# Two of three matrix products of a mixture layer by seven products on token halves, with its weight sums kept in DRAM

## Chip, core and metric

The kernel runs on one core of a Trainium2 chip. The metric is the device time of one execution in microseconds; several runs are taken, and their median counts. One execution was also profiled; all rows below are of that one.

## The reference

Attention in two steps (32 packed queries per head attend to the sequence, then the sequence attends to the 32 results), its output laid out as 4608 tokens of 512, and two feed-forward layers. The second is the one that is changed. Its weights and those of the first come as float64.

```python
p_packed = sm_attn(p, k, v)
out = sm_attn(q, p_packed, p_packed)                 # 8 batches, 8 heads, 576 tokens, 64
x = out.transpose(0, 2, 1, 3).reshape(4608, 512)
h = x @ w_in                                          # 512 -> 2048
g = np.where(h > 0.0, h, np.exp(np.minimum(h, 0.0)) - 1.0)
x2 = g @ w_out                                        # 2048 -> 512
a, b = x2 @ w_a, x2 @ w_b                             # 512 -> 1536 each
result = (a * b) @ w_out2                             # 1536 -> 512
```

## The kernel before

**Arithmetic.** Each large product is made of values split in two fp32r parts, hi and lo, and three matmuls (hi x hi, hi x lo, lo x hi) stand for one. Making a hi part is a cast on ACT, making the lo part a subtraction on DVE or POOL (`split`, L78; `convert`, L118 to L151). A float64 weight tile of 128 x 512 comes in as pairs of 32-bit words (512 KB, `load_words`), and `convert` makes it float32 with ACT, DVE and POOL steps u0 to u2; u3 makes hi and lo.

**Phase 1** goes batch by batch (eight blocks, about 85 us each from block 1 on; 288 tokens are one half of a batch). For each half and each of 16 pieces f of the hidden 2048, `l1` makes h (L466, 6 matmuls of 288 columns), `act1` makes g from it (ACT L474 and L475, DVE L478 for gf, ACT L480 and DVE L482 for gr) and `l2` adds its 12 matmuls into the four x2a banks (L488), two steps later. The attention of the next batch runs between these steps. Its work is put at due times: `put(t, fn)` queues a function for step time t, `run_until(t)` issues what has come due, with 2 time units for one step (h, f). The softmax over the packed keys (L331 to L358) and the transposes of the next batch's keys (L222) are DVE work of this kind. x2 goes to DRAM (x2d) as transposed tokens.

**Phase 2** takes nine blocks of 512 tokens and twelve pieces f of the hidden 1536. `l3` makes a and b of a piece (L727, 12 matmuls of 512 columns each), ACT copies a (L733), DVE multiplies by b (L735), and the product is split into cr (ACT L79, DVE L80). `l4` of the piece before adds its 12 matmuls into four banks o (L747). After piece 11 ACT and DVE copy the four banks into output tiles, which have two buffers (L758, L760), and SP stores them.

**Weights of phase 2.** There are 36 tiles (a, b, o of each f). All stay in SBUF, in slots that come free as phase 1 ends, so nine are converted during block 7 and 27 at the start of phase 2 (the list `convs`, at times T7 and T8, where the first unit of block 7 and the end of phase 1 lie).

The order on each engine is that of a scheduler that works from the program's order; a DMA issue on SP waits in line like any instruction.

## Time and profile before

| | us |
|---|---|
| median of 3 runs (lowest, highest) | 1731.46 (1731.41, 1734.84) |
| the profiled execution | 1731.33 |
| its span, first to last instruction | 1729.6 |
| PE busy, DVE busy, ACT busy, POOL busy | 1653.1, 796.5, 664.0, 160.7 |
| mean granted TensorE clock | 0.977 |

Busy times are sums over the span, and stages differ: POOL is busy only in the first stage and around the seam of the phases, DVE more in phase 1 than in phase 2. Matmuls are pipelined: the length of one in the profile holds time that it shares with its neighbours, so a pace is read from the starts of groups. Line numbers are those of the code above.

### The profile page before, as it was taken

The numbers are of one execution on the slowest core, as the hardware profiler recorded it, in microseconds if no ns is written. First come the engines' busy times: TensorE is split into PE (matmuls) and PEld (weight loads), VectorE is DVE, ScalarE is ACT, GpSimd is POOL, SyncE is SP. The second block draws the span as 40 slices with busy tenths as digits, with TensorE's granted clock in tenths as the row PEclk, the third lists the DMA queues.
The fourth block names the chain that finished last, engine by engine and source line by source line (L and its number), as shares of the span: only waits on it lengthen the run. The fifth ranks groups of instructions, "written<-read, shape, count | busy, mean of one in ns | idle before, by whom it ended". The sixth has DMA issues, their size and how long they took to land.

```text
span 1729.6 us, 25599 instructions
## 1 busy us (share of the span) xinstructions
PE 1653.1 (96%) x10392; PEld 1407.3 (81%) x10392; DVE 796.5 (46%) x1579; ACT 664.0 (38%) x1440; POOL 160.7 (9%) x124
## 2 busy tenths in 40 slices
PE   5489999999999999999989999999999999999998
PEld 3378889898989899898768888888888888888886
DVE  6998674656565655786892121221212121121211
ACT  4575655555656565565432121211212121121111
POOL 2564000000000000232450000000000000000000
PEclk7599999999999999999989999999999999999999
DMA  7754222223232221022531010010101000000000
GB/s 219 191 153 118 61 56 59 54 57 56 57 56 57 56 79 34 26 87 93 165 119 52 1 43 7 6 43 0 49 1 49 1 25 25 0 31 1 25 0 25
DMA packets 194806, 96.82 MB, mean 56 GB/s; under 512 B 147584, under 2 KB 179328, under 8 KB 194688
## 3 DMA queue, kind: packets, MB, share of 16 engines
q1 hardware_dynamic: 194688, 95.19, 20.2%
...
## 4 chain that ended last, share of the span: by engine, by line
PE 80%; DVE 12%; DMA 3%; issue 2%; SPq 1%; ACT 1%; POOL 1%; DVEq 0%; ACTq 0%; POOLq 0%
PE x2a L488 18%; PE o L747 17%; PE a L727 16%; PE b L727 16%; PE h L466 9%; DVE gf L478 1%; PE pp L294 1%; DVE kT L222 1%; DVE gr L482 1%; DMA wst_2b<-in_moe_w_b_dram 1%; DMA wst_i<-in_moe_w_in_dram 1%; DVE qT L222 1%; DVE wm_2b L135 0%; DVE t L337 0%; DMA wst_o<-in_moe_w_out_dram 0%
## 5 line engine op out<-in xcount | busy, mean ns | idle before, releaser
L488 PE MATMUL x2a<-gr,wout 128*128 128x288 f32 x3072 | 473.0, 300 | 10.6 <-DVE gr L482 6.6
L488 PEld LDWEIGHTS x2a<-gr,wout 128*128 128x128 f32 x3072 | 428.8, 190 | 43.4 <-issue 17.8
L735 DVE TENSOR_TENSOR cf<-asb,b 128x512 f32<-128x512 f32 x108 | 74.2, 687 | 533.1 <-PE b L727 532.4
L466 PE MATMUL h<-a,wr 128*128 128x288 f32 x1536 | 260.5, 304 | 21.8 <-DVE gf L478 14.1
L466 PEld LDWEIGHTS h<-a,wr 128*128 128x128 f32 x1536 | 222.8, 192 | 44.1 <-DVE gf L478 20.6
L733 ACT COPY asb<-a 128x512 f32<-128x512 f32 x108 | 63.4, 587 | 388.8 <-PE a L727 388.8
L727 PE MATMUL a<-x2r,wout 128*128 128x512 f32 x864 | 209.0, 391 | 0.0
L727 PEld LDWEIGHTS a<-x2r,wout 128*128 128x128 f32 x864 | 163.0, 189 | 35.9
L478 DVE SCALAR_TENSOR_TENSOR gf<-ge,h 128x288 f32<-128x288 f32 x256 | 114.6, 448 | 138.4 <-ACT ge L475 135.9
L79 ACT CAST cr<-cf 128x512 fp32r<-128x512 f32 x108 | 67.0, 620 | 249.2 <-DVE cf L735 249.2
L480 ACT CAST gr<-gf 128x288 fp32r<-128x288 f32 x256 | 110.3, 431 | 119.9 <-DVE gf L478 119.1
L474 ACT ACTIVATE ge<-h 128x288 f32<-128x288 f32 x256 | 104.9, 410 | 134.0 <-PE h L466 133.6
L482 DVE TENSOR_TENSOR gr<-gf,gr 128x288 fp32r<-128x288 f32 x240 | 115.4, 481 | 69.2 <-ACT gr L480 67.4
L747 PE MATMUL o<-wr,cr 128*128 128x512 f32 x540 | 138.9, 406 | 8.3 <-DVE cr L80 4.8
L747 PEld LDWEIGHTS o<-wr,cr 128*128 128x128 f32 x540 | 103.7, 193 | 35.3 <-DVE cr L80 6.5
L727 PE MATMUL b<-x2r,wr 128*128 128x512 f32 x540 | 129.8, 389 | 0.0
L727 PEld LDWEIGHTS b<-x2r,wr 128*128 128x128 f32 x540 | 101.4, 188 | 21.0
L475 ACT ACTIVATE ge<-ge 128x288 f32<-128x288 f32 x256 | 113.7, 445 | 5.5
L747 PE MATMUL o<-wout,cr 128*128 128x512 f32 x432 | 107.2, 396 | 0.2 <-DVE cr L80 0.2
L727 PE MATMUL a<-x2r,wx 128*128 128x512 f32 x432 | 104.2, 390 | 0.0
L80 DVE TENSOR_TENSOR cr<-cf,cr 128x512 fp32r<-128x512 f32 x108 | 76.8, 711 | 58.8 <-ACT cr L79 58.8
L727 PE MATMUL b<-x2r,wout 128*128 128x512 f32 x432 | 103.8, 389 | 0.0
...
## 6 DMA issues: line engine op xcount, KB each, us to landing
...
v<-in_v_dram SPq DMA_DIRECT2D x8, 1024.0 KB, 5.7
wst_i<-in_moe_w_in_dram SPq DMA_DIRECT2D x16, 512.0 KB, 5.3
wst_o<-in_moe_w_out_dram SPq DMA_DIRECT2D x16, 512.0 KB, 4.1
kst<-in_k_dram SPq DMA_DIRECT2D x112, 72.0 KB, 2.4
qst<-in_q_dram SPq DMA_DIRECT2D x112, 72.0 KB, 2.4
wst_2a<-in_moe_w_a_dram SPq DMA_DIRECT2D x12, 512.0 KB, 4.3
```

The source lines that it names most:

```text
L79: nc.scalar.copy(hi, src)
L80: nc.vector.tensor_tensor(lo, src, hi.bitcast(F32), op=ALU.subtract)
L466: nc.tensor.matmul(t[:, :HS], w[:, wi, o * P:(o + 1) * P], x[:, xi, :], start=(n == 0), stop=(n == 5))
L474: nc.scalar.activation(e, t[:, :HS], AF.Relu, scale=-1.0)
L475: nc.scalar.activation(e, e, AF.Exp, scale=-1.0)
L478: nc.vector.scalar_tensor_tensor(g, e, -1.0, t[:, :HS], op0=ALU.add, op1=ALU.max)
L480: nc.scalar.copy(gr[:, 0, :], g)
L482: (nc.gpsimd if pool_lo else nc.vector).tensor_tensor(gr[:, 1, :], g, gr[:, 0, :].bitcast(F32), op=ALU.subtract)
L488: nc.tensor.matmul(acc[d][:, :HS], wout_r[f][:, wi, d * P:(d + 1) * P], gr[:, xi, :], start=(first and n == 0), stop=(last and n == 2),)
L727: nc.tensor.matmul(t, w[:, wi, d * P:(d + 1) * P], xr[blk, d][:, xi, :], start=(n == 0), stop=(n == 3 * NDM - 1))
L735: nc.vector.tensor_tensor(c, a, ab[1], op=ALU.mult)
L747: nc.tensor.matmul(acc[t], cr[:, xi, t * P:(t + 1) * P], w[:, wi, :], start=(f == 0 and n == 0), stop=(f == NF2 - 1 and n == 2),)
```

## The change

Phase 2 is rewritten. Tokens are taken in six groups of 768, two halves of 384. For each piece f, [x2 halves] x [w_a | w_b] is a product of 2 x 2 blocks (two token halves, two halves of the 512 input channels; a and b). Strassen's scheme in Winograd's form makes the four block results from seven block products instead of eight: each product is one combination of token blocks (seven tensors s, made once a group) times one combination of weight blocks (seven tensors e, made once for each f). A product is six matmuls of 384 columns (two channel pieces of 128, three hi/lo terms). Sums of products are built in three PSUM banks A, B, C and on DVE (u, v, w), and then c1 = a x b of one half and c2 of the other are split as before. `l4` uses c1 of three token tiles right after, the tiles of c2 and the rest in a tail of 117 matmuls at the end of a group.

All 36 weight tiles are converted to float32 in blocks 1 to 6 of phase 1, one each 10 units, and stored in DRAM (wf). In group 0 the combinations e of a piece are made from them (`e_make`: 4 subtractions on DVE, 3 casts on ACT, 3 subtractions on POOL), stored in DRAM (ed, 1792 KB for each f), and groups 1 to 5 load them again (`e_load`, two buffers). Some buffers of the conversions in block 0 are also taken from other pools.

```diff
+            def u4():
+                nc.sync.dma_start(store, m.bitcast(F32))
...
+        GAP = (T7 - 4 * NF - 24) / len(w2src)
...
+        def w2_step(i, n):
+            kind, f, _ = w2src[i]
+            if n == 0:
+                w2words[i] = convert(w2words[i], f"2{kind}{f}", (stage, 2), store=wf[kind, f])
+            w2words[i][n]()
+
+        for i in range(len(w2src)):
+            t = 4 * NF + 12 + GAP * i
+            put(t - 7, w2_load, i)
+            for n, dt in enumerate((0, 1, 2, 5)):
+                put(t + dt, w2_step, i, n)
...
+        def e_load_words(f):
+            for kind in "ab":
+                t = stage.tile([P, 512], F32, tag="wmag", name=f"wl{kind}{f}", bufs=2)
+                nc.sync.dma_start(t, wf[kind, f])
+                wst2[kind, f] = t
+
+        def e_make(f):
+
+            a, b = wst2.pop(("a", f)), wst2.pop(("b", f))
+            e = p2.tile([P, 7, 2, 2 * P], F32R, tag="e2", name=f"e2_{f}", bufs=2)
+            c = stage.tile([P, 4, 2 * P], F32, tag="wst", name=f"wc{f}")
+            h1, h2 = slice(0, 2 * P), slice(2 * P, 4 * P)
+            nc.vector.tensor_tensor(c[:, 0, :], b[:, h1], a[:, h1], op=ALU.subtract)
+            nc.vector.tensor_tensor(c[:, 1, :], b[:, h2], b[:, h1], op=ALU.subtract)
+            nc.vector.tensor_tensor(c[:, 2, :], b[:, h2], c[:, 0, :], op=ALU.subtract)
+            nc.vector.tensor_tensor(c[:, 3, :], a[:, h2], c[:, 2, :], op=ALU.subtract)
+            for i, n, src in ((0, 2, a.rearrange("p (n x) -> p n x", n=2)), (2, 1, b[:, None, h2]), (3, 4, c)):
+                nc.scalar.copy(e[:, i:i + n, 0, :], src)
+                nc.gpsimd.tensor_tensor(e[:, i:i + n, 1, :], src, e[:, i:i + n, 0, :].bitcast(F32), op=ALU.subtract)
+            nc.sync.dma_start(ed[f], e.bitcast(F32))
+            es[f] = e
...
+        def e_load(f, g):
+            e = p2.tile([P, 7, 2, 2 * P], F32R, tag="e2", name=f"e2_{g}_{f}", bufs=2)
+            nc.sync.dma_start(e.bitcast(F32), ed[f])
...
+        def s_part(g, i, src):
+            s = p2.tile([P, 2, 2 * HT], F32R, tag=f"s{i}", name=f"s{i}_{g}")
+            split(s[:, 0, :], s[:, 1, :], src)
...
+            if step == 0:
+                s_part(g, 1, x11)
+                s1 = stage.tile([P, 2 * HT], F32, tag="wst", name=f"x2s1_{g}")
+                xs[g, "s1"] = s1
+                nc.vector.tensor_tensor(s1, x21, x22, op=ALU.add)
+                nc.vector.tensor_tensor(x21, x11, x21, op=ALU.subtract)
+                nc.vector.tensor_tensor(x11, s1, x11, op=ALU.subtract)
+                s_part(g, 6, x11)
+            elif step == 1:
+                s_part(g, 5, xs[g, "s1"])
+                s_part(g, 2, x12)
+                s_part(g, 7, x21)
+            else:
+                nc.vector.tensor_tensor(x12, x12, x11, op=ALU.subtract)
+                s_part(g, 3, x12)
+                s_part(g, 4, x22)
...
+        put(T7 + 4, e_load_words, 0)
+        put(T7 + 14, e_make, 0)
+        put(T7 + 20, e_load_words, 1)
+        put(T7 + 30, e_make, 1)
+        put(T7 + 36, e_load_words, 2)
+        put(T7 + 36, x_load, 0)
+        for n in range(3):
+            put(T7 + 46 + 4 * n, s_make, 0, n)
...
+        def o_load(f):
+            t = p4.tile([P, 512], F32, tag="wol", name=f"wlo{f}")
+            nc.sync.dma_start(t, wf["o", f])
+            w = p4.tile([P, 2, 512], F32R, tag=f"wo{f}", name=f"wo{f}", bufs=1)
+            nc.scalar.copy(w[:, 0, :], t)
+            nc.gpsimd.tensor_tensor(w[:, 1, :], t, w[:, 0, :].bitcast(F32), op=ALU.subtract)
+            wo[f] = w
...
+        def product(bank, f, i, first=True):
+            n = 0
+            for k in range(2):
+                for wi, xi in ((0, 0), (0, 1), (1, 0)):
                     nc.tensor.matmul(
...
+                        bank[:, :HT],
+                        es[f][:, E_OF[i], wi, k * P:(k + 1) * P],
+                        ss[i][:, xi, k, :],
+                        start=(first and n == 0),
+                        stop=(n == 5),
+                        skip_group_check=True,
                     )
...
+                    n += 1
...
+            product(bA, f, 1)
+            nc.scalar.copy(p1, pA)
+            product(bB, f, 6)
+            nc.vector.tensor_tensor(u, p1, pB, op=ALU.add)
+            product(bC, f, 5)
+            nc.scalar.copy(p5, pC)
+            product(bA, f, 2, False)
+            product(bB, f, 7, False)
+            nc.vector.tensor_tensor(v, p1, pB, op=ALU.add)
+            product(bC, f, 3, False)
+            nc.vector.tensor_tensor(u, u, pC, op=ALU.add)
+            nc.vector.tensor_tensor(u, u, pA, op=ALU.mult)
+            product(bB, f, 4, False)
+            nc.vector.tensor_tensor(w, p1, pB, op=ALU.add)
+            c1 = halves("c1", u, 2)
+            nc.vector.tensor_tensor(v, v, p5, op=ALU.add)
+            nc.vector.tensor_tensor(w, w, v, op=ALU.mult)
+            c2 = halves("c2", w, NF2)
+            return c1, c2
...
+        with tc.manual_schedule(engines={mybir.EngineType.PE}):
+            for g in range(NG):
+                c1, c2 = {}, {}
+                acc = [bank2("acc", f"o{g}_{t}", TT) for t in range(TT)]
+                for f in range(NF2):
+                    if g == 0:
+                        o_load(f)
+                        if f + 2 < NF2:
+                            e_make(f + 2)
+                        if f + 3 < NF2:
+                            e_load_words(f + 3)
+                    c1[f], c2[f] = l3(g, f)
+                    if g and f + 2 < NF2:
+                        e_load(f + 2, g)
+                    if f:
+                        for t in range(TT):
+                            l4(acc[t], c1[f - 1], t, f - 1)
+                    if f == NF2 - 2 and g + 1 < NG:
+                        x_load(g + 1)
+                if g + 1 < NG:
+                    for f in range(2):
+                        e_load(f, g + 1)
+                    for n in range(3):
+                        s_make(g + 1, n)
+                acc2 = bank2("A", f"o{g}_{TT}", 2)
+                for f in range(NF2 - 1):
+                    l4(acc2, c2[f], 0, f)
+                for t in range(TT):
+                    l4(acc[t], c1[NF2 - 1], t, NF2 - 1)
+                    out_rows(g, t, acc[t])
+                l4(acc2, c2[NF2 - 1], 0, NF2 - 1)
+                out_rows(g, TT, acc2)
+                for t in range(1, TT):
+                    acc2 = bank2("acc", f"o{g}_{TT + t}", TT)
+                    for f in range(NF2):
+                        l4(acc2, c2[f], t, f)
+                    out_rows(g, TT + t, acc2)
```

**TensorE in phase 2.** Before, from the l4 of one piece to the l3 of the next (o: output banks, wx: an output weight, x2r: tokens, wout and wr: slots that hold w_a and w_b):

```order
L747 MATMUL o_0_14677<-wx_9163,cr_2_14723 128x512 x3
L747 MATMUL o_1_14678<-wx_9163,cr_2_14723 128x512 x3
L747 MATMUL o_2_14679<-wx_9163,cr_2_14723 128x512 x3
L747 MATMUL o_3_14680<-wx_9163,cr_2_14723 128x512 x3
L727 MATMUL a_4_14783<-x2r_0_14236,wout_80 128x512 x3
L727 MATMUL a_4_14783<-x2r_1_14554,wout_80 128x512 x3
L727 MATMUL a_4_14783<-x2r_2_14557,wout_80 128x512 x3
L727 MATMUL a_4_14783<-x2r_3_14560,wout_80 128x512 x3
L727 MATMUL b_4_14796<-x2r_0_14236,wr_0_102 128x512 x3
```

Now, a piece of group 1 (s: token combinations, e: weight combinations, A, B, C: banks; L800 is `product`, L844 `l4`):

```order
L800 MATMUL A_3_12089<-s_1_11703,e_1_3_12002 128x384 x6
L800 MATMUL B_3_12090<-s_1_11710,e_1_3_12002 128x384 x6
L800 MATMUL C_3_12091<-s_1_11713,e_1_3_12002 128x384 x6
L800 MATMUL A_3_12089<-s_1_11716,e_1_3_12002 128x384 x6
L800 MATMUL B_3_12090<-s_1_11719,e_1_3_12002 128x384 x6
L800 MATMUL C_3_12091<-s_1_11723,e_1_3_12002 128x384 x6
L800 MATMUL B_3_12090<-s_1_11726,e_1_3_12002 128x384 x6
L844 MATMUL o_0_11867<-wo_10767,c_1_2_12070 128x512 x3
L844 MATMUL o_1_11868<-wo_10767,c_1_2_12070 128x512 x3
L844 MATMUL o_2_11869<-wo_10767,c_1_2_12070 128x512 x3
```

Before, three more rows of b follow. Where 24 matmuls of 512 columns and four output tiles stood, 42 of 384 columns and three output tiles stand; bank B takes product 7 in the fifth row and product 4 in the seventh, with one row between.

**VectorE in block 3 of phase 1**, in a stretch where the next batch's softmax (t, mx, a_4) stands beside gf and gr. Before:

```order
L478 SCALAR_TENSOR_TENSOR gf_1_2_5109<-ge_1_2_5104,h_1_2_5097 128x288
L337 TENSOR_TENSOR t_4992<-t_4992,mx_1_0_5219 128x288
L80 TENSOR_TENSOR wr_0_98<-wp_0__5345,wr_0_98 128x512
L358 TENSOR_TENSOR a_4_0_0_5116<-t_4992,a_4_0_0_5116 128x288
L337 TENSOR_TENSOR t_4992<-t_4992,mx_1_1_5227 128x288
L482 TENSOR_TENSOR gr_1_1_5071<-gf_1_1_5069,gr_1_1_5071 128x288
L358 TENSOR_TENSOR a_4_0_1_5152<-t_4992,a_4_0_1_5152 128x288
L482 TENSOR_TENSOR gr_1_2_5111<-gf_1_2_5109,gr_1_2_5111 128x288
L344 TENSOR_REDUCE mx_1_0_5219<-t_4992 128x9
```

Now (L139, L140 and L143 are the steps of `convert`, with wm_2b and wm_2o tiles of phase 2's weights; the other lines have moved down by seven):

```order
L485 SCALAR_TENSOR_TENSOR gf_1_2_5307<-ge_1_2_5300,h_1_2_5293 128x288
L344 TENSOR_TENSOR t_5183<-t_5183,mx_1_0_5420 128x288
L139 TENSOR_SCALAR wm_2b_5458<-wm_2b_5458 128x512
L344 TENSOR_TENSOR t_5183<-t_5183,mx_1_1_5428 128x288
L83 TENSOR_TENSOR wr_0_101<-wp_0__5556,wr_0_101 128x512
L365 TENSOR_TENSOR a_4_0_0_5314<-t_5183,a_4_0_0_5314 128x288
L139 TENSOR_SCALAR wm_2o_5638<-wm_2o_5638 128x512
L489 TENSOR_TENSOR gr_1_1_5265<-gf_1_1_5263,gr_1_1_5265 128x288
L365 TENSOR_TENSOR a_4_0_1_5352<-t_5183,a_4_0_1_5352 128x288
L140 TENSOR_SCALAR wm_2b_5458<-wm_2b_5458 128x512
L489 TENSOR_TENSOR gr_1_2_5309<-gf_1_2_5307,gr_1_2_5309 128x288
L351 TENSOR_REDUCE mx_1_0_5420<-t_5183 128x9
```

Between gf_1_2 and the row of mx, three conversion steps of two weight tiles have come in, two of them ahead of the first gr and the third ahead of the second.

## Rows read from the trace of the kernel before

**Rows 1.** Page, part 4: shares of the span on the chain that ended last.

```profile
PE x2a L488 18%; PE o L747 17%; PE a L727 16%; PE b L727 16%; PE h L466 9%; DVE gf L478 1%; PE pp L294 1%; DVE kT L222 1%; DVE gr L482 1%; DMA wst_2b<-in_moe_w_b_dram 1%; DMA wst_i<-in_moe_w_in_dram 1%; DVE qT L222 1%; DVE wm_2b L135 0%; DVE t L337 0%; DMA wst_o<-in_moe_w_out_dram 0%
```

**Rows 2.** Timeline, PE: start, length, engine, line, operation, out<-in, count.

```profile
1004.33 2.88 PE L727 MATMUL b<-x2r,wout 128*128 128x512 f32 x12
1007.05 2.97 PE L747 MATMUL o<-wr,cr 128*128 128x512 f32 x12
1009.86 1.31 PE L727 MATMUL a<-x2r,wout 128*128 128x512 f32 x5
```

**Rows 3.** Timeline, PE, in block 7 of phase 1.

```profile
714.57 0.96 PE L466 MATMUL h<-a,wr 128*128 128x288 f32 x6
715.37 1.76 PE L488 MATMUL x2a<-gr,wout 128*128 128x288 f32 x12
716.97 0.96 PE L466 MATMUL h<-a,wr 128*128 128x288 f32 x6
```

**Rows 4.** Waits of PE in 170:690, 690:820 and 815:1730: total, times, longest.

```profile
PE x2a L488 <- DVE x2s L506: 1.8, 4, 0.5
...
PE x2a L488 <- DVE gr L482: 5.0, 4, 2.6
PE h L466 <- DVE gf L478: 3.1, 4, 1.4
...
PE o L747 <- DVE cr L80: 5.0, 4, 2.3
PE o L747 <- ACT cr L79: 3.5, 2, 2.0
```

**Rows 5.** Stretches: length, busy of PE, PEld, DVE, ACT, POOL, clock, DMA share, GB/s.

```profile
865.00:868.00 3.00, 2.27 (x5) 1.82 (x6) 3.00 (x9) 1.18 (x2) 0.63 (x1) 0.50 0.21 74
```

**Rows 6.** Timeline, PE, in brackets the idle time before and its releaser.

```profile
865.73 4.63 PE L747 MATMUL o<-wr,cr 128*128 128x512 f32 x10 [2.34 <-DVE cr L80]
```

**Rows 7.** Groups by shape in 690:905, DVE and POOL: busy, mean ns, idle before.

```profile
L135 DVE TENSOR_SCALAR wm_2b<-wm_2b 128x512 f32<-128x512 f32 x12 | 10.6, 882 | 0.1
...
L139 DVE SCALAR_TENSOR_TENSOR wm_2b<-wst_2b,wm_2b 128x512 uint32<-128x512 uint32 x12 | 8.2, 680 | 0.0
...
L136 DVE TENSOR_SCALAR wm_2b<-wm_2b 128x512 uint32<-128x512 uint32 x12 | 7.2, 602 | 0.2
...
L147 DVE TENSOR_TENSOR wout<-wm_2a,wout 128x512 fp32r<-128x512 f32 x4 | 6.7, 1684 | 0.4 <-ACT wout L146 0.4
...
L142 POOL TENSOR_TENSOR wm_2b<-wm_2b,wst_2b 128x512 int32<-128x512 int32 x12 | 17.8, 1484 | 48.0 <-ACT cr L79 24.1 <-DVE wm_2b L139 16.1 <-ACT ge L475 3.3
```

**Rows 8.** Stretches, columns as in rows 5: a softmax stretch and a whole block.

```profile
500.00:510.00 10.00, 9.13 (x71) 7.43 (x71) 10.00 (x24) 6.34 (x17) 0.00 (x0) 1.00 0.60 129
...
605.00:690.00 85.00, 84.89 (x751) 77.42 (x750) 46.40 (x113) 50.41 (x124) 0.00 (x0) 1.00 0.16 52
```

**Rows 9.** Page, part 5: DVE groups at 288 and 512 columns.

```profile
L735 DVE TENSOR_TENSOR cf<-asb,b 128x512 f32<-128x512 f32 x108 | 74.2, 687 | 533.1 <-PE b L727 532.4
...
L478 DVE SCALAR_TENSOR_TENSOR gf<-ge,h 128x288 f32<-128x288 f32 x256 | 114.6, 448 | 138.4 <-ACT ge L475 135.9
...
L80 DVE TENSOR_TENSOR cr<-cf,cr 128x512 fp32r<-128x512 f32 x108 | 76.8, 711 | 58.8 <-ACT cr L79 58.8
```

**Rows 10.** Page, part 6: DMA issues, count, KB each, median us to landing.

```profile
v<-in_v_dram SPq DMA_DIRECT2D x8, 1024.0 KB, 5.7
...
wst_o<-in_moe_w_out_dram SPq DMA_DIRECT2D x16, 512.0 KB, 4.1
```

**Rows 11.** Timeline, DVE, beside rows 2 and 6.

```profile
1007.32 0.69 DVE L735 TENSOR_TENSOR cf<-asb,b 128x512 f32<-128x512 f32 x1 [6.20 <-PE b L727]
...
865.00 0.68 DVE L80 TENSOR_TENSOR cr<-cf,cr 128x512 fp32r<-128x512 f32 x1
```

**Rows 12.** Timeline, DVE, the last copy of the program.

```profile
1725.97 0.69 DVE L758 COPY osb<-o 128x512 f32<-128x512 f32 x1 [2.52 <-DMA out_dram<-osb]
```

**Rows 13.** Stretches, columns as in rows 5: one microsecond of the start.

```profile
24.00:25.00 1.00, 1.00 (x12) 1.00 (x10) 1.00 (x1) 0.00 (x0) 1.00 (x1) 0.50 0.99 365
```

More of the change, by code (lines that the diff above doesn't have):

```diff
@@ L706, in program, with w2_load @@
-        for d in range(NDM):
-            put(T8 - 32 + 4 * (d // 2), x2_load, 0, d)
-            put(T8 - 30 + 4 * (d // 2) + d % 2, x2_split, 0, d)
+        T7, T8 = 4 * NF * (B - 1), 4 * NF * B
+        GAP = (T7 - 4 * NF - 24) / len(w2src)
+        w2words = {}
+        def w2_load(i):
+            kind, f, src = w2src[i]
+            w2words[i] = load_words(src, f"2{kind}{f}")
+        def w2_step(i, n):
[3 more added lines that the diff above has]
+            w2words[i][n]()
@@ new lines, in program @@
+        for i in range(len(w2src)):
[3 more added lines that the diff above has]
+                put(t + dt, w2_step, i, n)
+        run_until(-1)
+        for b in range(B - 1):
+            m1_block(b)
+        run_until(T7 + 3)
+        at_stack.close()
+        p2 = ctx.enter_context(tc.tile_pool(name="p2", bufs=1, reuse_waits="tile"))
+        ps_a = ctx.enter_context(tc.tile_pool(name="ps_a", bufs=2, space=PSUM, side="right", reuse_waits="tile"))
@@ new lines, in program @@
+        E_OF = {1: 0, 2: 1, 3: 2, 5: 3, 7: 4, 6: 5, 4: 6}
+        ed = [dram.tile([P, 7, 2, 2 * P], F32, name=f"ed{f}") for f in range(NF2)]
+        wst2, es = {}, {}
+        xs, ss = {}, {}
+        def e_load_words(f):
[17 more added lines that the diff above has]
+            es[f] = e
@@ L712, in program @@
             run_pend()
+        ps_stack.close()
         m1_stack.close()
[L714 to L738 removed]
@@ new lines, in l4, with out_rows @@
+        def l4(acc, cr, t, f):
+            for n, (xi, wi) in enumerate(((0, 0), (0, 1), (1, 0))):
+                nc.tensor.matmul(
+                    acc,
+                    cr[:, xi, t * P:(t + 1) * P],
+                    wo[f][:, wi, :],
+                    start=(f == 0 and n == 0),
+                    stop=(f == NF2 - 1 and n == 2),
+                )
+        def out_rows(g, t, acc):
+            o = p4.tile([P, DM], F32, tag="osb", name=f"osb{g}_{t}")
+            if t % 2:
+                nc.vector.tensor_copy(o, acc)
+            else:
+                nc.scalar.copy(o, acc)
+            r0 = 2 * g * HT + t * P
+            nc.sync.dma_start(out[r0:r0 + P, :], o)
```

162 lines of the change are left out of this document (46 added, 116 removed).

## Prediction

> **What bounds the kernel now.** I read the chain that ended last first: its five matmul lines (x2a, o, a, b, h) make 18 + 17 + 16 + 16 + 9 = 76% of the span [rows 1]. So the kernel is a stream of matmuls on TensorE, and the questions are how long one lasts and where the stream breaks.
>
> How long: the pace, from start to start of neighbouring groups. In phase 2, 12 matmuls of the b product (512 columns) take 1007.05 - 1004.33 = 2.72 us and 12 of the output product 2.81 us [rows 2], that is 0.2267 and 0.234 us each. In phase 1 six h and twelve x2a matmuls of 288 columns stand between the starts 714.57 and 716.97 [rows 3]: 2.40 us for 18, 0.133 us each. (0.2267 - 0.1333) / 224 gives 0.417 ns a column, and a constant near 13 ns. The mean durations of the page (some 390 ns) overlap and are no pace.
>
> Where it breaks: not in blocks 1 to 6 (the largest sum of waits there is 1.8 us in 520), but in block 7, where PE waits 5.0 and 3.1 us for DVE, and at the head of phase 2, 5.0 us for DVE and 3.5 for ACT, which takes its input from DVE [rows 4]. Both have one cause: the second weights' conversions stand on DVE and POOL beside the work that PE waits for. After such a stall the granted clock is 0.50, the lower of its two levels, 1.2 GHz [rows 5], and ten matmuls take 4.63 us instead of some 2.4 [rows 6]; there are two such places, 865 and 889 us.
>
> **The change part by part**, against the profiled execution: span 1729.6, 1.7 us around it, 1731.3 in all, which is the median of the runs within 0.2 us.
>
> *The a and b products.* Before: 9 blocks x 12 f x 24 = 2592 matmuls of 512 columns, 2592 x 0.2267 = 587.6 us. After: 6 groups x 12 f x 7 products x 6 = 3024 of 384 columns. No row has 384 columns; the bounds are 0.133 (288) and 0.227 (512), and the straight line between them gives 0.1733, since both ends lie on one slope and run at the same clock: 524.1 us. **-63.5.** The output product stays at 1296 x 0.234 = 303 us: **0.**
>
> The Trainium skill has another rule (TensorE: Matmul & The Clock Gate, section Back-to-back issue gap): in a sustained stream one matmul takes about 81 ns at 128 columns and 131 ns at 512, so most of it doesn't depend on the columns. The trace doesn't agree: 227 ns at 512 and 133 at 288 [rows 2, 3]. An estimate by that page of the Trainium skill, 114 ns at 384, makes it 345 us instead of 340, no gain at all.
>
> *Conversions out of block 7 and out of the head of phase 2.* The waits of [rows 4] go: 8.1 us in block 7 and about 1 us at the lower clock behind the longest, 8.5 us in phase 2 and 2 x (4.63 - 2.4) = 4.5 us behind them. **-9.1 and -13.** What is late next there is new: block 7 makes the sums of weight pieces 0 and 1 and the first group's token sums. These are some 20 DVE operations on up to 768 columns where 9 conversions with their splits stood, so a third of the old stalls: **+3** (0 to 9).
>
> *All 36 conversions into blocks 1 to 6.* One conversion is on DVE three operations, 882 + 602 + 680 ns = 2.2 us by one weight's rows, and a POOL addition of 1.48 us [rows 7]; 36 x 2.2 = 78 us of DVE. A whole block has room: DVE is busy for 46.4 of 85 us [rows 8], and six conversions more make about 60. But it isn't even: as the heads of the next batch are softmaxed, DVE is busy for 10.00 of 10 us and PE only 9.13 [rows 8]. In the new order of DVE conversions come in threes, once in each half of a block, and in one half that is right in such a stretch: between the gf and gr that PE waits for stand conversion steps in rows where there were none. There the slack of PE is used up already, and DVE work put ahead of a gr is paid: of 3 x 2.2 = 6.6 us some two thirds stand ahead of a gr that is waited for, 4 us; the six other threes meet a DVE that is half idle and take perhaps 0.5 us. 6 x 4 = 24, and the others go into the upper bound. Bounds: nothing is paid but half a microsecond each (+5), or all of it and slower two-input operations beside POOL (+50). I take **+24**, the value nearest to the saturated row. The 36 stores to DRAM stand on SP behind POOL, with the next loads behind them; nothing of those is due within a block.
>
> The Trainium skill (SBUF — State Buffer, section SBUF: two separate sides) says that a DVE operation with two SBUF inputs and a GpSimd operation lock each other out for a whole instruction. The trace agrees in sign: the same subtraction is 711 ns in phase 2 and 1684 ns among the conversions [rows 7, 9]. An estimate by that page of the Trainium skill adds half of 36 x 1.48 us, some 27 us, to the 24.
>
> *Seam between the phases.* The first banks of phase 2 come free with the last copies of phase 1: one release, **+1.**
>
> *Group 0.* For each f the sums are made here: four DVE subtractions on 256 columns, three ACT casts, three POOL subtractions on 1792 columns in all (512 columns cost 1.48 us, so 5 us), and with the output weight's 6.5 of a 9.4 us step. Step: l3 42 x 0.1733 = 7.3, l4 9 x 0.234 = 2.1. The words of the next pair are loaded only as POOL lets the old ones go, and the subtractions on them stand on DVE ahead of v, for which product 4 waits. 512 KB land in 4.1 us and 1024 in 5.7 [rows 10]: 1.6 us for 512 KB and a fixed part of 2.5, so 3.3 for the words' 256 KB. From the end of one l3: cast and POOL 3.1 us, load 3.3, four subtractions 1.7, in all 8.1; v is due when five of the seven products are through and it has started, at 2.1 + 5/7 x 7.3 + 0.3 = 7.6 us. Late by 0.5 us in each of ten steps: **+5** (0 if the load takes 2.5; 20 if the subtractions run beside POOL at twice their time).
>
> *Groups 1 to 5.* Each f loads 128 x 3584 f32, 1792 KB, into one of two buffers, when l3(f) has let it go, for l3(f+2). The window is l4, l3, l4: 2.1 + 7.3 + 2.1 = 11.5 us. By the same slope it lands in 2.5 + 3.5 x 1.6 = 8.1 us. Covered by 3.4 us: **0.** If that cover goes it is the slower rival.
>
> *The wait of product 4 for v.* Products run on three banks; each bank's next product is two products off, 2.08 us, except that product 4 follows 7 in one bank with only product 3 between: 6 x 0.1733 = 1.04 us. In it v must be read: DVE starts 0.27 us behind the last matmul (12 from 1004.33 end at pace at 1007.05; it starts at 1007.32), PE 0.05 us behind DVE's end (865.68 and 865.73) [rows 2, 6, 11]; a 384-column operation that reads PSUM lies between 448 ns (288) and 687 (512) [rows 9], at 0.55. 0.87 of 1.04: hidden, margin 0.17. A wait of 0.1 to 0.2 us in 72 steps would be 7 to 14 us. **+1.** Other DVE work of a step: 5 x 0.55 + 4 x 0.58 = 5.1 of 9.4 us, covered.
>
> *Between groups.* 117 output matmuls (27 us) need none of the new token sums, which take 10.6 us of DVE (7 lo parts, 4 sums). One of them stands ahead of the last v of a group: 5 x 0.6, **+3.**
>
> *End.* The last copy waits 2.52 us for an output buffer to be stored [rows 12]; now output tiles come one by one, so that wait goes: **-2.7.**
>
> Sum: -63.5 - 9.1 - 13 - 2.7 + 3 + 24 + 1 + 5 + 1 + 3 = -51.3. Span 1678, with 1.7 around it **1680 us**.
>
> **The rivals.**
> 1. *All is hidden.* Conversions cost 5 instead of 24, group 0, the seams and v nothing: 1680 - 19 - 9 = 1652. For it: half of each block has an idle DVE. Against: the saturated 10 us rows. 0.12.
> 2. *The conversions and group 0 are paid in full*: 50 and 20 instead of 24 and 5, 1680 + 41 = 1721. For it: DVE at 1684 ns beside POOL. Against: so far PE loses only some half a microsecond in each saturated stretch, so there may be more slack than I count. 0.15.
> 3. *Slower: the reload doesn't land in its window.* With two buffers two steps last L + 7.3 us, L being the landing; over 18.8 it is paid, (L - 11.5) / 2 in each of 50 steps (the first two of a group load under the tail). L = 13.5 eats the 51 us, L = 16 gives 1680 + 112 = 1792. It decides when those 1.835 MB move at under 1.835 / (13.5 - 2.5) = 167 GB/s. Against: 365 GB/s in a microsecond of the start [rows 13], though that is of many small transfers at once. 0.08.
> 4. *No change: a 384-column matmul is not on the line.* At 0.190 us each, 3024 make 575, and the gain is gone: 1731. For it: no row has this width, and the upper bound of 0.227 would even be slower than before. Against: the line through two widths leaves little room between them. 0.03. The rule of the Trainium skill on the issue gap (TensorE: Matmul & The Clock Gate, section Back-to-back issue gap) would give this outcome; its figures don't fit either width here.
>
> **How the numbers follow.** Forecast 0.62 (1660 to 1705), rivals 0.12, 0.15, 0.08 and 0.03. The range, from rival 1 to rival 2, 1652 to 1721, leaves out rivals 3, 4 and what lies at the two ends' far sides, under 0.2. A difference under 0.2% can't be told from none by a measurement of this kernel. Faster: 0.62 + 0.12 + 0.15 = 0.89; same 0.03; slower 0.08.
>
> **What would show it.** A pace of 0.173 us for the 384-column matmuls; six stalls of some 4 us in blocks 1 to 6, ended by gr or gf on DVE, and an even stream elsewhere; no wait over 1 us of PE in block 7; in groups 1 to 5 a step of 9.4 us, no PE wait for a DMA, landings of the 1792 KB near 8 us. I am wrong if PE waits for the weight sums in groups 1 to 5, if product 4 waits for v in every step, or if the stalls of blocks 1 to 6 sum to under 5 or over 50 us.

## The result: 1672.6 us instead of 1732.9, and the profile after

The changed kernel takes 1672.61 us (median of 4 runs, 1672.34 to 1673.35) beside 1732.88 us of the kernel before in the same runs; the ratio is 0.9652, with an interval of 0.9635 to 0.9669. The profiled execution has a span of 1670.5 us instead of 1729.6: **-59.1 us**, where the forecast had -51.3.

The shares of the chain that ended last, from the page, beside [rows 1], and the line of the page on the reloads of weight sums (count, KB each, median us to landing):

```profile
PE x2a L495 18%; PE o L844 17%; PE B L800 12%; PE h L473 9%; PE C L800 8%; PE A L800 8%; POOL e L722 2%; DVE gf L485 1%; DVE kT L229 1%; DVE gr L489 1%; PE pp L301 1%; DMA wst_2o<-in_moe_w_out_dram 1%; DMA wst_i<-in_moe_w_in_dram 1%; DVE t L344 1%; DMA wst_o<-in_moe_w_out_dram 1%
```

```profile
e<-ed SPq DMA_DIRECT2D x60, 1792.0 KB, 7.1
```

A, B and C (L800, the seven products) now make 28% of the span where a and b made 32, and no DMA stands among the large lines. A step in group 3, from the timeline of PE and DVE (columns as in [rows 2]):

```profile
1170.10 2.25 PE L844 MATMUL o<-wo,c 128*128 128x512 f32 x9
...
1172.18 1.23 PE L800 MATMUL A<-s,e 128*128 128x384 f32 x6
...
1173.25 1.20 PE L800 MATMUL B<-s,e 128*128 128x384 f32 x6
...
1177.41 1.20 PE L800 MATMUL C<-s,e 128*128 128x384 f32 x6
1177.61 0.56 DVE L830 TENSOR_TENSOR v<-p,B 128x384 f32<-128x384 f32 x1 [2.50 <-PE B L800]
...
1178.45 1.21 PE L800 MATMUL B<-s,e 128*128 128x384 f32 x6
```

Between the starts of neighbouring products lie 1.04 us for six matmuls of 384 columns, 0.1733 us each (1.07 us for the first product, which follows output matmuls); the nine output matmuls take 2.08 us, 0.231 each. v starts 0.20 us after product 3 has started, ends at 1178.17, and product 4 starts on time at 1178.45. In groups 1 to 5 every step with output matmuls has this form: 9.40 us.

The waits of PE in blocks 1 to 6, block 7 with the seam, and the head of phase 2 (columns and stretches as in [rows 4]); from 950 us on there is none:

```profile
PE x2a L495 <- DVE gr L489: 6.6, 6, 1.9
PE h L473 <- DVE gf L485: 5.8, 6, 1.5
```

```profile
PE x2a L495 <- DVE gr L489: 1.6, 1, 1.6
PE h L473 <- DVE gf L485: 1.3, 2, 0.9
```

```profile
PE B L800 <- DVE v L830: 5.9, 4, 3.2
PE B L800 <- DVE u L825: 3.6, 8, 0.5
```

**Where the time went.** Phase 1 ends at its last x2a matmul. Before, that is 815.9 us: the first stretch of pure phase 2 begins at 823.60, and 34 matmuls of phase 2, 7.7 us, stand ahead of it. Now the last row of x2a ends, at its pace of 0.133 us, at 829.1, and six matmuls of phase 2 (from 797.87), 1.0 us, stand ahead of it, which makes 828.0:

```profile
824.27 4.92 PE L495 MATMUL x2a<-gr,wout 128*128 128x288 f32 x36
```

| stretch | before | after | difference | forecast |
|---|---|---|---|---|
| phase 1 up to the middle of block 6 (by its h matmuls) | - | - | +20.2 | +24 |
| from there to the last x2a matmul | - | - | -8.1 | -9.1 + 3 |
| l3: 2592 x 0.2271, now 3024 x 0.1740 | 588.6 | 526.2 | -62.4 | -63.5 |
| output matmuls: 1296 x 0.2343, now 0.2288 | 303.7 | 296.5 | -7.2 | 0 |
| the rest of phase 2: waits, restarts, lower clock | 14.8 | 16.0 | +1.2 | -13 + 10 |
| last matmul to the end of the span | 6.6 | 3.8 | -2.8 | -2.7 |

The first two lines compare the start of the same h matmul in both traces, and 0.2271, 0.1740, 0.2343 and 0.2288 are means over the matmuls after 960 us (of the 42 product matmuls of a step the first five take 0.175 to 0.185 us, the others 0.173 to 0.176). Runs of the same code in phase 1 differ by up to 2 us at the start of block 1, so differences of that size there say nothing.

### The profile page after: what moved, and what is told of

It reads as the page before. It is cut to its first block, busy times and chain, and to the rows that moved or that the text cites. A ratio compares the mean times of both kernels' runs of the same rounds, so it can differ in the third digit from the quotient of the medians.

```text
span 1670.5 us, 27502 instructions
## 1 busy us (share of the span) xinstructions
PE 1586.3 (95%) x10824; PEld 1443.7 (86%) x10824; DVE 1034.4 (62%) x2035; ACT 706.4 (42%) x1566; POOL 207.8 (12%) x154
## 4 chain that ended last, share of the span: by engine, by line
PE 75%; DVE 11%; issue 5%; DMA 3%; POOL 3%; ACT 3%; SPq 1%; DVEq 0%; ACTq 0%; POOLq 0%
PE x2a L495 18%; PE o L844 17%; PE B L800 12%; PE h L473 9%; PE C L800 8%; PE A L800 8%; POOL e L722 2%; DVE gf L485 1%; DVE kT L229 1%; DVE gr L489 1%; PE pp L301 1%; DMA wst_2o<-in_moe_w_out_dram 1%; DMA wst_i<-in_moe_w_in_dram 1%; DVE t L344 1%; DMA wst_o<-in_moe_w_out_dram 1%
## 5 line engine op out<-in xcount | busy, mean ns | idle before, releaser
L844 PE MATMUL o<-wo,c 128*128 128x512 f32 x1296 | 309.3, 393 | 0.0
L844 PEld LDWEIGHTS o<-wo,c 128*128 128x128 f32 x1296 | 243.5, 188 | 48.2
L800 PE MATMUL B<-s,e 128*128 128x384 f32 x1296 | 261.3, 336 | 9.8 <-DVE v L830 5.9
L800 PEld LDWEIGHTS B<-s,e 128*128 128x128 f32 x1296 | 226.7, 188 | 14.2 <-DVE v L830 7.2
L800 PE MATMUL A<-s,e 128*128 128x384 f32 x864 | 174.9, 337 | 0.2 <-ACT p L823 0.2
L800 PE MATMUL C<-s,e 128*128 128x384 f32 x864 | 173.0, 334 | 0.0
L800 PEld LDWEIGHTS A<-s,e 128*128 128x128 f32 x864 | 154.0, 188 | 6.4 <-ACT p L823 0.5
L800 PEld LDWEIGHTS C<-s,e 128*128 128x128 f32 x864 | 151.9, 188 | 0.0
L830 DVE TENSOR_TENSOR v<-p,B 128x384 f32<-128x384 f32 x72 | 39.9, 554 | 140.5 <-PE B L800 140.5
L825 DVE TENSOR_TENSOR u<-p,B 128x384 f32<-128x384 f32 x72 | 39.8, 553 | 104.1 <-PE B L800 104.1
```

The source lines that it names most:

```text
L800: nc.tensor.matmul(bank[:, :HT], es[f][:, E_OF[i], wi, k * P:(k + 1) * P], ss[i][:, xi, k, :], start=(first and n == 0), stop=(n == 5), sk ...
L825: nc.vector.tensor_tensor(u, p1, pB, op=ALU.add)
L830: nc.vector.tensor_tensor(v, p1, pB, op=ALU.add)
L844: nc.tensor.matmul(acc, cr[:, xi, t * P:(t + 1) * P], wo[f][:, wi, :], start=(f == 0 and n == 0), stop=(f == NF2 - 1 and n == 2),)
```

## The experiments

Spans are those of the profiled executions; 1670.5 is the changed kernel's.

**What the conversions cost in phase 1.** In the changed kernel each block from 2 on has two small stalls. One of them, in time order of POOL, DVE and PE:

```profile
476.08 1.32 POOL L146 TENSOR_TENSOR wm_2o<-wm_2o,wst_2o 128x512 int32<-128x512 int32 x1 [28.33 <-DVE wm_2o L143]
476.13 1.55 DVE L139 TENSOR_SCALAR wm_2a<-wm_2a 128x512 f32<-128x512 f32 x1 [0.28 <-ACT wm_2a L133]
...
478.57 0.83 PEld L473 LDWEIGHTS h<-a,wr 128*128 128x128 f32 x6 [1.36 <-DVE gf L485]
```

The conversion step of DVE (one input, float32) takes 0.43 us elsewhere, 1.55 while POOL adds; gf stands behind it, and PE waits for gf. The other stall, in block 3 (DVE and PE):

```profile
428.44 0.41 DVE L139 TENSOR_SCALAR wm_2b<-wm_2b 128x512 f32<-128x512 f32 x1
...
430.11 0.41 DVE L139 TENSOR_SCALAR wm_2o<-wm_2o 128x512 f32<-128x512 f32 x1
...
430.94 2.25 PE L495 MATMUL x2a<-gr,wout 128*128 128x288 f32 x15 [1.06 <-DVE gr L489]
```

Two conversion steps of 0.41 us stand in DVE's row ahead of the gr, with no POOL instruction beside them, and PE waits 1.06 us. This is the kind of stall that the prediction had, at a quarter of its size.

e1 leaves POOL's addition out:

```diff
-                nc.gpsimd.tensor_tensor(m.bitcast(I32), m.bitcast(I32), low.bitcast(I32), op=ALU.add)
+                if store is None:
+                    nc.gpsimd.tensor_tensor(m.bitcast(I32), m.bitcast(I32), low.bitcast(I32), op=ALU.add)
```

> The changed kernel without the POOL addition in the 36 conversions of blocks 1 to 6 (the low words are left out of the weights; all else is as it was). In the changed kernel these blocks are 20 us later than before, two stalls in each: about 1.06 us ended by gr and 1.17 us ended by gf. Theory 'POOL blocks DVE': a 0.43 us conversion step on DVE took 1.55 us exactly while such an addition ran, ahead of the gf that PE waited for; then the gf stalls go (6 x 1.2 = 7 us) and the gr stalls stay, span about 1663. Rival 'the amount of DVE work': nothing changes on DVE, span 1669 to 1671.

Span 1665.1 (-5.4). Waits of PE in 330 to 690 us:

```profile
PE x2a L496 <- DVE gr L490: 4.2, 4, 1.1
...
PE h L474 <- DVE gf L486: 0.9, 2, 0.7
```

From the start of block 3 to the middle of block 6 it loses 3.8 us to the kernel before, the changed one 7.1. The gf stalls are gone and the gr stalls stay: POOL blocks DVE here, and that is about half of the cost of these blocks, though 7 us were expected of it in all and 5.4 came.

e2 leaves the three DVE steps out:

```diff
             def u1():
+                if store is not None:
+                    return
```

(and u2's DVE step in the same way)

> The changed kernel without the three DVE steps in the 36 conversions of blocks 1 to 6 (weights come out as garbage; ACT steps, POOL addition, loads and stores stay). Theory 'DVE work ahead of gr and gf, and its blocking by POOL, is the whole cost of the conversions': blocks 1 to 6 fall back from +20 us to under +4, span about 1653. Rival 'loads, stores and ACT steps cost as much': at least 8 of the 20 us stay, span 1658 or more.

Span 1664.9 (-5.6): by its number the rival holds, 16 of the 20 us stay at the middle of block 6. This doesn't show that DVE's steps cost nothing, because POOL's additions stay, and without the steps they meet other DVE operations. The stretch of the stall above, in e2 (POOL, DVE):

```profile
424.95 1.33 POOL L149 TENSOR_TENSOR wm_2o<-wm_2o,wst_2o 128x512 int32<-128x512 int32 x1 [0.64 <-ACT wst_2o L136]
424.98 1.98 DVE L347 TENSOR_TENSOR t<-t,mx 128x288 f32<-128x288 f32 x2
```

Two softmax subtractions take 1.98 us instead of 0.44 and 0.45, and PE's wait for this gr grows from 1.06 to 1.55 us. No run leaves out both, so how much of the 20 us is DVE's own work stays open. What is left in e2 at the start of block 2, 6.0 us, has another place, and a row at the seam of blocks 0 and 1 shows it:

```profile
172.12 3.39 PE L498 MATMUL x2a<-gr,wout 128*128 128x288 f32 x12 [3.08 <-ACT gr L490]
```

PE waits for ACT's cast to gr. In the changed kernel the same place reads (ACT's conversion step, what it waited for, and PE):

```profile
167.03 0.68 ACT L133 ACTIVATE wm_2o<-wst_2o 128x512 f32<-128x512 f32 x1 [2.49 <-DMA wst_2o<-in_moe_w_out_dram]
...
173.96 0.79 PE L495 MATMUL x2a<-gr,wout 128*128 128x288 f32 x4 [0.91 <-ACT gr L487]
...
180.60 2.41 PE L495 MATMUL x2a<-gr,wout 128*128 128x288 f32 x12 [1.89 <-DVE gr L489]
```

ACT waits 2.49 us for the load of a weight, and 1.81 for the next (171.87), and the casts to gr are queued behind. PE's longest wait here, 1.89 us, is for a gr on DVE, which is busy without a break from 175 to 185 us.

e5 puts the loads earlier:

```diff
-            put(t - 7, w2_load, i)
+            put(t - 19, w2_load, i)
```

> The changed kernel with the 36 weight loads of phase 1 put 12 time units (about 17 us) earlier; nothing else differs. In the changed kernel ACT's first conversion step waits 8.3 us in all for these loads, with casts to gr queued behind it, most of it in block 1, where the whole block is 8.5 us later than before. Theory 'ACT waits for the load': those waits go and block 1 loses most of its 8.5 us, span 1660 to 1664. Rival 'DVE work and POOL's blocking are the whole cost': no change, 1669 to 1672. A third case: early loads hold the five buffers and queue on the DMA queue ahead of the key and query loads, and the span grows.

Span 1670.0, 1671.66 us in the runs: no change, but it didn't test the theory: the first loads came at most 9 us earlier instead of 17, ACT's steps on them moved forward too (that on wst_2o from 167.03 to 160.53), and ACT's waits for loads summed to 11 us instead of 8.3. That asked for another place, not another time:

e9 converts in blocks 2 to 6 (on top of e8, below):

```diff
-        GAP = (T7 - 4 * NF - 24) / len(w2src)
+        GAP = (T7 - 8 * NF - 24) / len(w2src)
...
-            t = 4 * NF + 12 + GAP * i
+            t = 8 * NF + 12 + GAP * i
```

> The kernel with POOL's pieces and the output weights' subtraction on DVE, and on top of it the 36 conversions in blocks 2 to 6 instead of 1 to 6 (one each 8.2 time units instead of 10). Against the changed kernel, block 1 is 8.5 us later than before the change, blocks 2 to 6 another 12. Theory 'block 1 is special: there the last loads of phase 1's own weights and partial sums hold the buffers, so that a load is issued 1.5 us ahead of its use and ACT waits': block 1 loses all of its cost, blocks 2 to 6 pay 36/30 of theirs, +2.4: span 1662.6 - 8.5 + 2.4 = 1656 to 1657. Rival 'the first three conversions cost that wherever they stand': no change, 1661 to 1664.

Span 1654.6 instead of e8's 1662.6; 1655.77 us in the runs, ratio 0.9555 (0.9538 to 0.9572). Waits of PE in 120 to 250 us, where block 1's price was:

```profile
PE x2a L495 <- POOL gr L489: 1.4, 2, 0.8
PE h L473 <- DVE gf L485: 0.4, 1, 0.4
```

Block 1 ends 0.7 us ahead of the kernel before (e8: 9.5 behind), blocks 2 to 6 cost 14.0 up to the middle of block 6, where 14.4 was expected. So 9 of the 20 us came from the place of the first conversions, block 1, and not from their being the first. What makes the place dear is not shown. In e9 ACT still waits for these weights' loads, 12.6 us in all in blocks 2 to 6 and up to 1.84 at a time, but PE waits for a gr of ACT only 0.2 us. And of the 9.0 us at the start of block 2, 7.2 stay without POOL's additions (e1) and 6.0 without the DVE steps (e2).

e10 halves POOL's addition on top of that:

```diff
-                nc.gpsimd.tensor_tensor(m.bitcast(I32), m.bitcast(I32), low.bitcast(I32), op=ALU.add)
+                for x in (slice(0, 256), slice(256, 512)) if store is not None else (slice(0, 512),):
+                    nc.gpsimd.tensor_tensor(m[:, x].bitcast(I32), m[:, x].bitcast(I32), low[:, x].bitcast(I32), op=ALU.add)
```

> The kernel with the conversions in blocks 2 to 6, POOL's pieces and the output weights' subtraction on DVE, and on top of it POOL's addition in each conversion cut into two of 256 columns. In blocks 2 to 6 PE waits 6.4 us for gf in five places of up to 1.7 us, where a conversion step on DVE of 0.43 us takes up to 1.55 beside an addition of 1.3 us. Theory 'DVE is blocked for one whole POOL instruction': with 0.7 us instructions these waits halve, 1652 to 1653 us of span. Rival 'DVE is blocked until POOL has run dry': no change, 1654 to 1656.

Span 1653.7, 1654.69 us, ratio 0.954 (0.9524 to 0.9556), which can't be told from e9. PE's waits for gf in 330 to 690 us went from 6.4 to 6.1, in five places of up to 1.6. The time is the rival's; the rows are not (POOL, DVE):

```profile
374.45 1.63 POOL L147 TENSOR_TENSOR wm_2o<-wm_2o,wst_2o 128x256 int32<-128x256 int32 x2 [30.37 <-DVE wm_2o L143]
374.51 0.97 DVE L139 TENSOR_SCALAR wm_2a<-wm_2a 128x512 f32<-128x512 f32 x1 [0.29 <-ACT wm_2a L133]
...
375.52 0.85 DVE L140 TENSOR_SCALAR wm_2a<-wm_2a 128x512 uint32<-128x512 uint32 x1
```

DVE's step is held up for one half only, 0.97 us instead of the 1.52 that it takes in e9, and ends while POOL has the second half to do. But the next step meets that half and takes 0.85 us instead of 0.43, so the two together take 1.82 us instead of 1.95, and the waits stay.

**Group 0.** The changed kernel in the step at 861 us (POOL, DVE, PE):

```profile
861.21 2.72 POOL L722 TENSOR_TENSOR e<-wc,e 128x1024 fp32r<-128x1024 f32 x1
...
861.58 2.75 DVE L83 TENSOR_TENSOR c<-w,c 128x384 fp32r<-128x384 f32 x1
...
863.88 3.01 POOL L789 TENSOR_TENSOR wo<-wlo,wo 128x512 fp32r<-128x512 f32 x2
...
864.73 1.02 DVE L716 TENSOR_TENSOR wc<-wlb,wla 128x256 f32<-128x256 f32 x1
...
865.67 1.50 DVE L717 TENSOR_TENSOR wc<-wlb 128x256 f32<-128x256 f32 x1
...
868.49 1.00 PEld L800 LDWEIGHTS B<-s,e 128*128 128x128 f32 x6 [1.57 <-DVE v L830]
```

DVE's subtraction with two inputs from SBUF takes 2.75 us, until POOL's of 2.72 us has ended (0.55 us in group 3); two word subtractions take 1.02 and 1.50 beside POOL's next pair (0.4 alone), v comes late, and PE waits 1.25 us. The words themselves are in time here: DVE waits for a load of them once in 826 to 950 us, 0.9 us.

The Trainium skill (SBUF — State Buffer, section SBUF: two separate sides) says that DVE and GpSimd share one port pair which one instruction holds to its end, against DVE operations with two SBUF inputs and those in a two-port mode. These rows agree: 2.75 us for 0.55 beside a POOL instruction of 2.72, and 1.55 for 0.43 beside one of 1.32. The second operation has one input; that it runs in a two-port mode is not seen in the trace.

e3 cuts POOL's work into pieces (the output weights' too, in two):

```diff
-                nc.gpsimd.tensor_tensor(e[:, i:i + n, 1, :], src, e[:, i:i + n, 0, :].bitcast(F32), op=ALU.subtract)
+                for j in range(n):
+                    nc.gpsimd.tensor_tensor(
+                        e[:, i + j:i + j + 1, 1, :], src[:, j:j + 1, :], e[:, i + j:i + j + 1, 0, :].bitcast(F32), op=ALU.subtract
+                    )
```

> The changed kernel with every POOL subtraction of group 0 cut into pieces of 256 columns (the same work in more instructions). In group 0 PE waits 5.9 us for v and 3.6 us for u, with about 1.5 us at the lower clock behind. Theory 'POOL blocks DVE': DVE subtractions of 0.67 us took 2.3 to 2.75 us beside the 1024-column POOL subtraction, and the word subtractions 1.0 to 1.5 instead of 0.4 beside the output weight's; in pieces the waits for u go and those for v fall to about 3, span about 1663 to 1665. Rival 'the words land late': the waits stay within 1 us of what they were, span 1669 to 1671.

Span 1668.4 (-2.1). In 826 to 950 us PE's waits for u went from 3.6 to 0.2 us, and those for v from 5.9 to 10.8, up to 3.3 at a time. One of the longer ones (DVE and PE):

```profile
896.91 0.42 DVE L716 TENSOR_TENSOR wc<-wlb,wla 128x256 f32<-128x256 f32 x1 [4.02 <-DMA wlb<-wfb]
...
898.99 2.29 PE L804 MATMUL B<-s,e 128*128 128x384 f32 x6 [2.59 <-DVE v L834]
```

The waits for u went, as the blocking has it. Those for v grew by the rival's cause: DVE waits for a load of words in seven places, 13.5 us in all where it was 0.9, and here the subtractions behind the load take 0.42 us, unblocked. The load is issued at 891.76, when POOL's subtraction on the last words (890.69, 1.05 us) has ended, and lands 5 us later. The gain, 4.3 us, is in block 7, where the first sums are made. Neither theory was right alone.

e4 loads the words from piece 3 on a step ahead:

```diff
-                t = stage.tile([P, 512], F32, tag="wmag", name=f"wl{kind}{f}", bufs=2)
+                if f < 3:
+                    t = stage.tile([P, 512], F32, tag="wmag", name=f"wl{kind}{f}", bufs=2)
+                else:
+                    t = p4.tile([P, 512], F32, tag="wl", name=f"wl{kind}{f}", bufs=4)
...
-                        if f + 3 < NF2:
-                            e_load_words(f + 3)
+                        if f == 0:
+                            e_load_words(3)
+                        if f + 4 < NF2:
+                            e_load_words(f + 4)
```

> The changed kernel with four more buffers for the words of weight pieces 3 to 11 in group 0, which are then loaded a step earlier; POOL's instructions are as they were. Rival 'the words land late' (the one the prediction was made by): v's waits go, span about 1664. Theory 'POOL blocks DVE': only the first v wait, 3.2 us, can shrink, the waits for u (3.6 us) stay, span 1667 to 1671.

Span 1676.9 (+6.4): v's waits fell to 4.5 us, those for u rose to 7.5. The word subtractions moved forward in DVE's row, ahead of u, w and the c subtractions. Of the 6.4 us, 2.8 lie in phase 1, where the code is the same, so the waits of group 0 are the firmer sign.

e8 adds to e3's pieces that the output weights' subtraction runs on DVE:

```diff
-            nc.gpsimd.tensor_tensor(w[:, 1, :], t, w[:, 0, :].bitcast(F32), op=ALU.subtract)
+            nc.vector.tensor_tensor(w[:, 1, :], t, w[:, 0, :].bitcast(F32), op=ALU.subtract)
```

> The changed kernel with POOL's subtractions for the weight sums in pieces of 256 columns and the output weights' subtraction moved from POOL to DVE. With the pieces alone the kernel gained 4 us in block 7, but in group 0 the waits for v grew from 5.9 to 10.8 us. Theory 'POOL's load of 8 of 9.4 us in the first six steps, which blocks the word subtractions ahead of v': with 5 us of POOL a step the v waits fall under 6 us, span 1661 to 1665. Rival 'the words themselves land late': v waits stay at 9 or more, span 1667 to 1671.

Span 1662.6, 1665.73 us: the time is in the range of the theory, the waits for v are 7.4 us instead of under 6. What they end on is another thing now (SP's issue of the word load, the word subtraction, PE):

```profile
866.29 0.32 SPq L707 DMA_DIRECT2D wlb<-wfb  x1
...
870.36 0.42 DVE L716 TENSOR_TENSOR wc<-wlb,wla 128x256 f32<-128x256 f32 x1 [2.20 <-DMA wlb<-wfb]
...
872.49 1.32 PE L803 MATMUL B<-s,e 128*128 128x384 f32 x6 [1.64 <-DVE v L833]
```

DVE waits 2.20 us for the load, 4 us after its issue. As in e3, that is the mechanism of the prediction: it sets in once POOL's long instructions are out of the way.

e12 gives the words from piece 3 on buffers of their own, on top of e9:

```diff
-                t = stage.tile([P, 512], F32, tag="wmag", name=f"wl{kind}{f}", bufs=2)
+                if f < 3:
+                    t = stage.tile([P, 512], F32, tag="wmag", name=f"wl{kind}{f}", bufs=2)
+                else:
+                    t = p4.tile([P, 512], F32, tag="wl", name=f"wl{kind}{f}", bufs=4)
```

> The kernel with the conversions in blocks 2 to 6, POOL's pieces and the output weights' subtraction on DVE (1655.8 us), and on top of it four buffers of their own for the words of weight pieces 3 to 11, so that their load doesn't wait for POOL's subtraction on the last pair. With POOL unloaded, DVE waits 2.2 us for a word load ahead of v and PE 1.64 us for v, in eight steps 7.2 us in all. Theory 'now the words are late, as the prediction had it': these waits fall under 3 us, span 1649 to 1652. Rival 'the word subtractions, moved forward in DVE's row by the earlier loads, get in the way elsewhere' (as when the words were only loaded a step ahead): waits for v and u stay at 6 or more, span 1654 or more.

Span 1659.3, 1660.63 us, 5 us slower than e9: the rival's time. In 826 to 950 us PE still waits 6.9 us for v and 2.1 for u. But the theory wasn't tested, because the load still waits for POOL (SP's issue, DVE):

```profile
883.51 0.32 SPq L710 DMA_DIRECT2D wlb<-wfb  x1
...
887.76 0.42 DVE L719 TENSOR_TENSOR wc<-wlb,wla 128x256 f32<-128x256 f32 x1 [3.12 <-DMA wlb<-wfb]
```

It is issued when POOL's subtraction on an earlier pair (882.43, 1.06 us) has ended, DVE waits 3.12 us for it, and PE 1.69 us for the v behind. How group 0 could do without these waits stays open.

**The reload.** e6 issues each reload twice:

```diff
-            nc.sync.dma_start(e.bitcast(F32), ed[f])
+            for _ in range(2):
+                nc.sync.dma_start(e.bitcast(F32), ed[f])
```

> The changed kernel with each of the 60 reloads of weight sums issued twice into the same buffer, so that the landing L grows from 7.1 us to 12 (side by side) or 14.2 us (one after the other). By the prediction's window of 11.5 us the cost is (L - 11.5) / 2 in each of 50 steps: 12 or 13 us at L = 12 (span 1683), 68 us at L = 14.2 (span 1738, slower than before). Rival 'the window is wider because a late load eats into the slack of the next one': under half of that.

Span 1836.0 (+165.5), slower than before the change. The second load waits for the first, and each lands in 7.7 us, so L is at least 15.4; the formula gives (15.4 - 11.5) / 2 x 50 = 98 us. PE's waits after 950 us, and what follows one of them:

```profile
PE A L801 <- DMA e<-ed: 106.0, 37, 5.5
```

```profile
1174.63 2.29 PE L801 MATMUL A<-s,e 128*128 128x384 f32 x6 [4.62 <-DMA e<-ed]
1176.72 2.12 PE L801 MATMUL B<-s,e 128*128 128x384 f32 x6
1178.64 2.12 PE L801 MATMUL C<-s,e 128*128 128x384 f32 x6
1180.56 1.35 PE L801 MATMUL A<-s,e 128*128 128x384 f32 x6
```

The waits are 106 us, near the formula. The other 60 are the restart: after this wait of 4.62 us eighteen matmuls take 2.1, 1.9 and 1.9 us for six instead of 1.04, at a granted clock of 0.50. Over 985 to 1832 us the granted clock is 0.93 in the mean, and the missing 7% of 847 us is 59 us. The clock behind that wait:

```profile
1174.00:1177.00 3.00, 2.37 (x7) 2.37 (x8) 0.00 (x0) 0.00 (x0) 0.00 (x0) 0.50 0.98 421
```

**The wait for v.** e7 adds a copy ahead of v:

```diff
+            nc.vector.tensor_copy(w, pB)
             nc.vector.tensor_tensor(v, p1, pB, op=ALU.add)
```

> The changed kernel with one more DVE copy of 384 columns from the bank of product 7 ahead of v in every step (0.55 us, some 0.48 behind another operation). In groups 1 to 5 v ends 0.28 us before product 4 starts, so product 4 should be late by 0.2 to 0.27 us in 60 steps and a little more in group 0: +13 to +20 us, span 1684 to 1690. Rival 'product 4 has more slack than the rows show': under 3 us.

Span 1698.8 (+28.3). A step of group 3, in which the copy starts at 1200.49 (DVE and PE):

```profile
1200.96 0.54 DVE L831 TENSOR_TENSOR v<-p,B 128x384 f32<-128x384 f32 x1
...
1201.56 1.01 PEld L800 LDWEIGHTS B<-s,e 128*128 128x128 f32 x6 [0.39 <-DVE v L831]
...
1202.74 2.25 PE L845 MATMUL o<-wo,c 128*128 128x512 f32 x9
```

Product 4 starts 1.27 us after product 3 (1200.29) instead of 1.04, 0.23 late, as expected; but its six matmuls then take 1.18 us, and a step is 9.75 us instead of 9.40. A wait of 0.23 us costs 0.35, 21 us in 60 steps; the other 7 fall in group 0. So the whole is over the 13 to 20 us that were expected.

**The output matmuls.** They were faster than before, which nobody had forecast. At the end of a group (PE):

```profile
1226.52 28.78 PE L844 MATMUL o<-wo,c 128*128 128x512 f32 x126
1255.13 1.20 PE L800 MATMUL A<-s,e 128*128 128x384 f32 x6
```

126 in 28.61 us, 0.227 each, where the nine of a step take 0.231. e11 lets two steps pass before a c tile is read:

```diff
-            c1 = halves("c1", u, 2)
+            c1 = halves("c1", u, 3)
...
-                    if f:
+                    if f > 1:
...
-                            l4(acc[t], c1[f - 1], t, f - 1)
+                            l4(acc[t], c1[f - 2], t, f - 2)
...
+                    l4(acc[t], c1[NF2 - 2], t, NF2 - 2)
```

> The changed kernel with the output matmuls of a piece issued two steps behind its products instead of one (c1 in three buffers; the tail of a group grows from 117 to 126 matmuls). In the changed kernel the nine output matmuls of a step take 0.232 us each and the 126 at a group's end 0.227 from the tenth on; before, the twelve took 0.234. Theory 'freshly written c tiles cost PE a few ns each': all output matmuls go at 0.227, a step falls from 9.40 to 9.35 us, span 1668. Rival 'it is their place right behind the products, whatever they read': the steps stay at 9.40 us, span 1670.5 within 1.

Span 1676.0; the steps stay at 9.40 us, the nine at 2.09 (PE):

```profile
1173.40 2.25 PE L844 MATMUL o<-wo,c 128*128 128x512 f32 x9
1175.49 1.23 PE L800 MATMUL A<-s,e 128*128 128x384 f32 x6
```

So it isn't the age of the tiles. It goes with their place behind the products: the first nine of the 126 take 0.232 us each as well, and 117 of 216 output matmuls of a group now stand behind such nine in one row. Why PE takes a few ns more there wasn't found, nor how long it lasts: before, all twelve of a row take 0.231 to 0.238. The span's +5.5 us lie in phase 1 (2 us), in group 0 and in the first steps of the groups, where products now follow each other without output matmuls between.

## Why the prediction was right, point by point

- **The products** (-63.5): right, -62.4. The straight line between 288 and 512 columns gave 0.1733 us, and 0.1740 was measured in the mean; the difference is in the first five matmuls behind output matmuls. The issue-gap rule of the Trainium skill (TensorE: Matmul & The Clock Gate, section Back-to-back issue gap), 114 ns by the estimate made from it, doesn't hold for this kernel's matmuls.
- **Output matmuls** (0): mis-sized, -7.2; the tail's row is faster.
- **Block 7 and the head of phase 2** (-9.1 + 3 and -13): -8.1 and -14.8, right in size. One sign failed: in block 7 PE waits 1.6 us once, for gr, where no wait over 1 us was to be. And POOL's long subtractions still cost 4.3 us there (e3).
- **Conversions in blocks 1 to 6** (+24): the size is near, +20.2, and the step to it failed. "DVE work put ahead of a gr is paid" was to give six stalls of 4 us in the saturated stretches. There were none of 4 us. Some 9 us came from the place of the first conversions, block 1 (e9); why it is dear there is open, since ACT's waits for loads, which the rows suggest, come again in e9 without the cost. The rest are two stalls of about 1.1 us a block: one is POOL blocking DVE (e1), the other, by its rows, DVE work ahead of a gr, as forecast but of 1.06 us. A price worked out from the busy share of one engine hit the sum by luck.
- **Group 0** (+5, with 0 to 20): mis-sized, and by the wrong cause. Waits of 9.9 us and slower matmuls behind them make 16.0 us with the seam, where 6 were forecast. The 5 were for words that land late; in the changed kernel DVE waited 0.9 us for them. What made v and u late were POOL's long subtractions, which the prediction had for this stage only as its upper bound of 20. The late words are real but second in line: they come out when POOL's instructions are cut or moved (13.5 us of DVE's waits in e3, 10.7 in e8).
- **The reload** (0): right. It lands in 7.1 us (8.1 estimated) of 11.5, and no wait is seen. Its rival had the right mechanism and waits (106 us measured for 98 by formula), but the price left out the restart: break-even is nearer than L = 13.5.
- **v** (+1): right, 0. The margin is 0.28 us between v's end and product 4; an operation of 0.47 us ahead of v used it up and made product 4 0.23 late (e7).
- **Between groups** (+3): 0. The token sums' operations ahead of the last v don't delay it.
- **End** (-2.7): right, -2.8.

The errors, -7.2 (output), -3.8 (conversions), -3 (between groups), -3.8 (block 7 and the head), -1.1 (v and end), +1.1 (products) and +10.0 (group 0 and the seam), add up to the 7.8 us between forecast and result. So the sum is nearer than its parts, and that too is luck. Rival 1's terms beside the conversions add up to 10, not 9, which moves its 1652 by 1 us.
